# Storing one tile's blocks earlier and turning q in two halves, in a linear attention and expert kernel

## The chip, the cores and the metric

The kernel runs on one core of a Trainium2 chip. The metric is the device time of one execution in microseconds (us). Five engines work side by side and meet at semaphores: TensorE (PE) multiplies, VectorE (DVE), ScalarE (ACT) and GpSimd (POOL) compute elementwise, and SyncE (SP) issues most of the transfers (DMAs). Each engine takes its instructions strictly in the order in which the program lists them.

## The reference

Eight batches of linear attention, whose output is the input of four experts that every row goes through:

```python
# q, k, v: (8, 8 heads, 576, 64)
phi = lambda x: np.where(x > 0, x, np.exp(x) - 1.0) + 1.0
q_p, k_p = phi(q), phi(k)
kv  = einsum('bhsd,bhse->bhde', k_p, v);  z = sum(k_p, axis=2)
num = einsum('bhsd,bhde->bhse', q_p, kv)
den = einsum('bhsd,bhd->bhs', q_p, z)[..., None] + 1e-06
x = (num / den) as rows of 8 * 64            # 4608 x 512
# domain_probs: (4608, 4), w1: (4, 512, 1024), w2: (4, 1024, 512)
p = domain_probs / (domain_probs.sum(-1, keepdims=True) + 1e-09)
out = sum over e of p[:, e:e+1] * (maximum(x @ w1[e], 0.0) @ w2[e])
```

## The kernel before

**Tiles.** A tile is 512 rows of `x`: 512 of the 576 rows of one batch; the 64 left over of each of the eight batches make a ninth tile (`xT_left`). Tiles run in the order 0 to 6, the ninth, 7. While the experts of one tile run on PE, the attention of the next batch runs on the other engines and in gaps that are made for it in PE's order, so that its `x` is ready, transposed, when the next tile begins.

**The experts of a tile.** For each of the four experts, layer 1 (`Block`, lines 875 to 949) and layer 2 (`layer2_product`, line 807; for tile 0 `layer2_part`, line 732) run as blocks of four or eight matmuls. Both layers after tile 0 use a scheme with seven products in place of eight, for which POOL makes sums (`hidden_sum`, `token_sum`). A result of layer 2 is added into `acc`, a block of 128 rows by 512: the first time by ACT (line 726), after that by DVE (line 728). A tile has four such blocks. `acc` has five buffers (`NACC`), and one of them serves a piece of q early in the program. When the last expert's part is added, the block is stored by a DMA that SP issues (`store`, line 709); the buffer is free for another block when that store has landed.

**The attention of a batch.** q, k and v come as four pieces each (two heads, 256 KB) into a ring of six buffers (`raw`, lines 324 to 342), and the 64 rows left over in separate small loads ("rests", `load_left`, line 310, two DMAs each for k, v and q). ACT and DVE compute phi in two steps: `phi_act` (lines 364 and 367) writes x + 1 into `kp` or `qp` and exp(x) into PSUM, `phi_dve` (line 372) combines them. `kv` multiplies. q has to be turned (transposed) to be a weight of PE: for batches 2 to 7 one DMA transposes all of `qp` into `qT` (`dma_qT`, line 410); for batch 1 PE does it (`pe_qT`, line 445). `nd` (line 487) multiplies `qT` by `kvz` in six groups of three, each followed by a division on DVE into `x_sb`; `dma_xT` turns each finished pair of heads into the next tile's `xT`.

**The order.** Every step is a named generator, put at a position counted in slots (56 slots a tile, from `CFG["ATTN"]` for the attention), and the steps are sorted by position: that is the order of instructions on each engine. For the first two tiles, up to a part of batch 3's steps, the order is written out by hand, `CFG["EARLY"]`: each appearance of a name advances its generator to the next `yield`. So `y3.23`, layer 2 of tile 0 for expert 3, block 2, part 3, appears three times: matmuls, the addition on DVE, the store. Names that matter here: `y3.03`, `y3.13`, `y3.23`, `y3.33` (blocks 0 to 3 of tile 0); `m10.21` and the like (tile 1, expert 0, product 2, half 1); `b2.q1` and `b2.qm1` (batch 2, `phi_act` and `phi_dve` of q's piece 1); `b2.load3` (a load into the ring); `b1.next` (the rests of batch 2); `b2.qT` (turning); `b2.nd0` (first group of numerators).

Of the kernel before, what the change touches and what calls it, by code (L numbers as in the profile page):

```python
# [12 lines left out]
FP16 = mybir.dt.float16  # L13
# [17 lines left out]
            v=(18.1, 19.16, 22.55, 30.55),  # L31
            k=(-5.5, 26.3, 27.5, 28.5),
# [5 lines left out]
            q=(36.4, 36.95, 40.2, 43.4),  # L38
            qd=(37.75, 39.0, 40.55, 44.7),
            lq=54.05,  # L40
            lqd=54.5,
# [9 lines left out]
            v=(4.4, 8.7, 12.1, 14.8),  # L51
            k=(0.3, 2.9, 6.7, 11.25),
# [5 lines left out]
            q=(20.1, 22.1, 27.0, 30.0),  # L58
            qd=(21.75, 27.2, 30.2, 32.3),
            lq=33.9,  # L60
            lqd=38.3,
            qT=35.9,
            nd=(39.3, 40.4, 42.0, 43.5, 45.3, 46.1),
            nl=52.1,
        ),
# [1 line left out]
            v=(4.4, 8.7, 12.1, 14.8),  # L67
            k=(0.3, 2.9, 6.7, 11.25),
# [5 lines left out]
            q=(20.1, 22.1, 27.0, 30.0),  # L74
            qd=(21.75, 27.2, 30.2, 32.3),
            lq=23.3,
            lqd=24.4,
            qT=35.9,
            nd=(39.3, 40.4, 42.0, 43.5, 45.3, 46.1),
            nl=37.2,  # L80
        ),
# [53 lines left out]
    ),  # L135
}

# [2 lines left out]
def kernel(  # L140
# [10 lines left out]
    nc = tc.nc  # L151
    ATTN, HSUM, L2ORD, L2AT = (CFG[x] for x in ("ATTN", "HSUM", "L2ORD", "L2AT"))

    B, H, S, D = q.shape
# [72 lines left out]
    def aps(shape, dtype, name, more=""):  # L227
        return ppm.tile(shape, dtype, tag=CFG["BANK"].get(now[0] + more, "s"), bufs=2, name=name)
# [67 lines left out]
    class Batch:  # L296
# [59 lines left out]
        def phi_act(self, name, i):  # L356

            if name == "k" and self.kp is None:
                self.kp = pa.tile([P, CM, H, D], FP16, tag="kp", bufs=1, name="kp")
            if name == "q" and self.qp is None:  # L360
                self.qp = pa.tile([P, CM, H, D], FP16, tag="kp", bufs=1, name="qp")
            src = self.raw[name, i]
            dst = (self.qp if name == "q" else self.kp)[:, :, i * HQ : (i + 1) * HQ, :]
            nc.scalar.activation(dst.rearrange("p c h d -> p h c d"), src, AF.Identity, bias=1.0)
            ee = aps([P, HQ * CM * D], FP32, "psum_ee")
            ee = ee.rearrange("p (c h d) -> p c h d", c=CM, h=HQ)
            nc.scalar.activation(ee.rearrange("p c h d -> p h c d"), src, AF.Exp)
            self.ph[name, i] = dst, ee
# [38 lines left out]
                    out=dst, in0=dst, scalar=1.0, in1=el[us], op0=AO.max, op1=AO.min  # L407
                )

        def dma_qT(self):  # L410
            if self.qT is None:
                self.qT = pa.tile([P, CM, NPAIR, P], FP16, tag="qT", bufs=1, name="qT")
            nc.sync.dma_start_transpose(
                out=self.qT.rearrange("p c a i -> p (c a) i"),
                in_=self.qp.rearrange("p c h d -> p (c h d)"),
            )

        def dma_qTl(self):
# [25 lines left out]

        def pe_qT(self, pair, eng=nc.vector):
            ps = aps([P, CM, P], FP16, "psum_qT")
            for c in range(CM):
                nc.tensor.transpose(
                    out=ps[:, c], in_=self.qp[:, c, 2 * pair : 2 * pair + 2], identity=identh
                )  # L450
            yield
            if self.qT is None:
                self.qT = pa.tile([P, CM, NPAIR, P], FP16, tag="qT", bufs=1, name="qT")
            (eng.copy if eng is nc.scalar else eng.tensor_copy)(out=self.qT[:, :, pair], in_=ps)

        def kv(self):
            ps = aps([P, NPAIR, DE], FP32, "psum_kv")
# [29 lines left out]
        def nd(self, i0, n):  # L487

            ps = aps([P, 3, 2, DE], FP32, "psum_nd")
            for i in range(n):  # L490
                pair, c = divmod(i0 + i, CM)
                nc.tensor.matmul(  # L492
                    out=ps[:, i],
                    lhsT=self.qT[:, c, pair],
                    rhs=self.kvz[:, pair],
                    start=True,
                    stop=True,
                )
            yield
            if self.x is None:  # L500
                x = pa.tile([P, CM, H, DE], FP16, tag="vp", bufs=1, name="x_sb")
                x = x.rearrange("p c h d -> p (c h d)")[:, 0 : NPAIR * CM * P]
                self.x = x.rearrange("p (a c i) -> p a c i", c=CM, i=P)
            self.norm(self.x.rearrange("p a c i -> p (a c) i")[:, i0 : i0 + n], ps, n)
# [450 lines left out]
    def batch_steps(bt, nxt, put, at, at_next):  # L955
# [6 lines left out]
            if m < len(later):  # L962
                (bt if m < len(mine) else nxt).load(*later[m])

        def load_left():
            if nxt is not None:
                nxt.alloc_left()
                nxt.load_left("k", "v", "q")

        b = bt.b  # L970

# [19 lines left out]
            put(at["l" + n], f"b{b}.l{n}", bt.left_act, n)  # L991
            put(at["l" + n + "d"], f"b{b}.l{n}m", bt.left_dve, n)
        put(at["kv"], f"b{b}.kv", bt.kv)
        put(at["lqd"] + 1, f"b{b}.next", load_left)
        if not first:
            put(at["lqd"] + 2, f"b{b}.qTl", bt.dma_qTl)
        if first:
            put(at["qtl"], f"b{b}.qTl", bt.pe_qTl)
            for i in range(NPAIR):
                put(at["qt"][i], f"b{b}.qT{i}", bt.pe_qT, i, nc.scalar)  # L1000
                for hf in range(2):
                    put(at["nd"][i], f"b{b}.nd{i}{hf}", bt.nd, i * CM + 2 * hf, 2)
                put(at["xt"][i], f"b{b}.xT{i}", bt.pe_xT if i == 2 else bt.dma_xT, i)
            for i in range(NRAW):
                put(at["next"][i], f"b{b}.load{i}", load, len(mine) + i)
        else:
            put(at["qT"], f"b{b}.qT", bt.dma_qT)
            for i in range(6):
                put(at["nd"][i], f"b{b}.nd{i}", numerators, 3 * i, min(3, NPAIR * CM - 3 * i))
        if nxt is None or b in (1, 4):  # L1010
# [17 lines left out]
    with tc.manual_schedule(  # L1028
# [76 lines left out]
        for j in range(0, NTILES - 1):  # L1105
            at = base + 2 * NSLOT * E * (j - 1) if j else 0.0

            def put(pos, *g, at=at):
                put_at(at + pos, *g)
# [65 lines left out]
```

## Time and profile before

| | |
|---|---|
| median of three runs | 486.1 us |
| the three runs | 484.93, 486.1, 487.2 us |
| the profiled execution | 484.29 us |
| its span, first to last instruction | 482.5 us |
| granted clock of PE | 0.999 |

Lines of a profile read so: the start in us from the span's start and the duration, the engine (SPq is SP's queue of issues, PEld the loading of weights into PE), the line of the kernel, the operation, what it writes and what it reads, the shapes, the number of instructions merged, and in brackets how long the engine stood idle before and what ended that by the profile's inference. Lines on DMAs give the number of issues, the size of one and the median time from issue to landing. A table by stretches gives the window, its length, then the busy time (and the number of instructions) of PE, PEld, DVE, ACT and POOL, PE's granted clock, the busy share of the DMA engines and their GB/s.

### The profile page before, as it was taken

Reading aid. Unit: us, or ns where it says so; the run is one execution under the profiler, and the core shown is the slowest. Engines: PE = TensorE matmul, PEld = TensorE weight load, DVE = VectorE, ACT = ScalarE, POOL = GpSimd, SP = SyncE. Lnnn points to the kernel's source line nnn. Section 1 sums busy time; section 2 is a strip of 40 time slices with the busy share of each in tenths; the row PEclk is TensorE's granted clock in tenths of the full one; section 3 lists DMA queues with packets and bytes.
Section 4 is the critical chain, followed back from the end, with each engine's and each line's share of the span. In section 5 each row is a group of like instructions: output and inputs, shape, how many; then the busy total and the mean of one; then the engine's idle time right before and its main releaser. Section 6 shows DMA issues by size and latency. Waiting matters only on the chain.

```text
span 482.5 us, 12014 instructions
## 1 busy us (share of the span) xinstructions
PE 475.3 (98%) x4565; PEld 407.1 (84%) x4565; DVE 379.1 (79%) x794; ACT 329.8 (68%) x659; POOL 358.8 (74%) x343
## 2 busy tenths in 40 slices
PE   8999999999999999999999999999999999999997
PEld 3776757898889888998889888988898888888886
DVE  5868998897968796888678885988787756775677
ACT  5688969956795599649874888478954465446540
POOL 5566144788966986789777976697769877987775
PEclk9999999999999999999999999999999999999999
DMA  8999997533445155524552346423230020003002
GB/s 293 218 218 259 234 200 234 154 84 88 132 145 108 43 157 160 122 59 117 178 135 57 109 131 161 83 67 113 67 70 13 1 88 1 1 2 88 2 1 87
DMA packets 80297, 54.06 MB, mean 112 GB/s; under 512 B 45344, under 2 KB 72992, under 8 KB 80240
## 3 DMA queue, kind: packets, MB, share of 16 engines
q1 hardware_dynamic: 70096, 40.89, 31.3%
q0 software_dynamic: 8896, 11.34, 12.1%
q10 hardware_dynamic: 1248, 1.08, 0.7%
q8 instruction: 35, 0.57, 0.5%
q14 instruction: 22, 0.18, 0.1%
HBM read 45.16 MB, written 9.44 MB: 113 GB/s over the span
## 4 chain that ended last, share of the span: by engine, by line
PE 94%; DMA 2%; DVE 2%; ACT 1%; issue 0%; SPq 0%; ACTq 0%
PE py L832 38%; PE pb L889 25%; PE pe L889 19%; PE py L737 6%; PE ph L677 1%; PE psum_nd L492 1%; DMA rawq<-in_q_dram 1%; PE psum_kv L464 1%; DMA out_dram<-acc 1%; PE pb L832 1%; PE pe L832 1%; PE psum_nl L511 0%; DVE acc L728 0%; DVE kpos L588 0%; ACT ee L603 0%; ACT acc L726 0%
## 5 line engine op out<-in xcount | busy, mean ns | idle before, releaser
L728 DVE SCALAR_TENSOR_TENSOR acc<-py,p_sb,acc 128x256 f32<-128x256 f32 (+1 forms) x382 | 182.1, 488 | 43.9 <-PE py L832 39.4
L873 DVE CUSTOM_DVE_ANT_0 h<-pe,u 128x512 f16<-128x512 f32 x140 | 96.0, 688 | 43.3 <-PE pe L889 22.5
L889 PEld LDWEIGHTS <-w 128*128 128x128 f16 x1120 | 109.0, 98 | 16.1
L799 POOL TENSOR_TENSOR hs<-h 128x512 f16<-128x512 f16 x64 | 73.8, 1154 | 56.0 <-DVE h L873 44.3
L832 PEld LDWEIGHTS <-h 128*128 128x128 f16 x1024 | 99.9, 98 | 12.3 <-issue 0.9
L832 PE MATMUL py<-w,h 128*128 128x256 f16 x744 | 106.5, 273 | 0.6 <-ACT acc L726 0.6
L900 ACT COPY u<-pb 128x512 f32<-128x512 f32 x140 | 82.7, 592 | 30.9 <-PE pb L889 28.6
L801 POOL TENSOR_TENSOR hs<-hs,h 128x512 f16<-128x512 f16 x64 | 74.3, 1160 | 24.9 <-PE py L832 22.3
L889 PEld LDWEIGHTS <-s 128*128 128x128 f16 x840 | 81.4, 98 | 11.6
L889 PE MATMUL pb<-tt,w 128*128 128x256 f16 x560 | 83.9, 273 | 0.0
L832 PEld LDWEIGHTS <-hs 128*128 128x128 f16 x768 | 74.3, 98 | 8.9 <-issue 0.2
L805 POOL TENSOR_TENSOR hs<-h,hs 128x512 f16<-128x512 f16 x64 | 74.7, 1167 | 1.2 <-POOL h L803 0.7
L803 POOL TENSOR_TENSOR h<-h 128x512 f16<-128x512 f16 x64 | 74.3, 1161 | 0.1
L832 PE MATMUL py<-t,hs 128*128 128x256 f16 x496 | 74.1, 273 | 0.0
L922 ACT ACTIVATE h<-pe 128x512 f16<-128x512 f32 x70 | 42.1, 601 | 41.8 <-PE pe L889 41.3
L915 ACT COPY pe<-pb 128x512 f32<-128x512 f32 x70 | 40.0, 573 | 39.8 <-PE pb L889 14.5
L943 ACT ACTIVATE h<-pb 128x512 f16<-128x512 f32 x70 | 41.9, 600 | 5.4 <-PE pb L889 5.4
L889 PE MATMUL pb<-tt,s 128*128 128x256 f16 x280 | 41.8, 273 | 0.0
L889 PE MATMUL pe<-tt,s 128*128 128x256 f16 x280 | 41.8, 273 | 0.0
L889 PE MATMUL pe<-xT,s 128*128 128x256 f16 x248 | 37.1, 273 | 0.0
L889 PE MATMUL pe<-xT,w 128*128 128x256 f16 x248 | 37.1, 273 | 0.0
L889 PE MATMUL pb<-xT,w 128*128 128x256 f16 x248 | 36.9, 273 | 0.0
(134 smaller groups left out, 594.8 us busy)
## 6 DMA issues: line engine op xcount, KB each, us to landing
w<-in_moe_w_dram POOLq DMA_DIRECT2D x14, 512.0 KB, 10.4
out_dram<-acc SPq DMA_DIRECT2D x28, 256.0 KB, 2.5
rawb<-in_k_dram SPq DMA_DIRECT2D x24, 256.0 KB, 3.1
rawb<-in_q_dram SPq DMA_DIRECT2D x24, 256.0 KB, 2.6
rawb<-in_v_dram SPq DMA_DIRECT2D x24, 256.0 KB, 2.7
out_dram<-acc SPq DMA_DIRECT2D x12, 128.0 KB, 2.3
w<-in_moe_w_dram POOLq DMA_DIRECT2D x4, 256.0 KB, 5.4
rawb<-in_k_dram POOLq DMA_DIRECT2D x4, 256.0 KB, 10.5
```

The costliest lines, as they stand in the source:

```text
L728: nc.vector.scalar_tensor_tensor(out=acc, in0=ps, scalar=pscal, in1=acc, op0=AO.mult, op1=AO.add)
L799: nc.gpsimd.tensor_tensor(out=hs[0], in0=a21, in1=a22, op=AO.add)
L801: nc.gpsimd.tensor_tensor(out=hs[1], in0=hs[0], in1=a11, op=AO.subtract)
L803: nc.gpsimd.tensor_tensor(out=a21, in0=a11, in1=a21, op=AO.subtract)
L805: nc.gpsimd.tensor_tensor(out=hs[3], in0=a12, in1=hs[1], op=AO.subtract)
L832: nc.tensor.matmul(out=ps, lhsT=lhsT(k), rhs=rhs[:, k], start=first and k == 0, stop=k == FH - 1, skip_group_check=True,)
L873: nc.vector._custom_dve(TENSOR_ADD_SAT, out=out, in0=ps, in1=u, s0=BIG, s1=0.0)
L889: nc.tensor.matmul(out=ps[:, kk], lhsT=lk(kc), rhs=rhs[:, kc], start=first and kk == 0 and kc == 0, stop=kc == 1, skip_group_check=True,)
L900: nc.scalar.copy(u, self.b)
L915: nc.scalar.copy(self.e5, self.b)
L922: nc.scalar.activation(self.h[:, :, 0, 0:NH], self.e5, AF.Relu)
L943: nc.scalar.activation(self.h[:, :, 1, 0:NH], self.b, AF.Relu)
```

## The change

Three edits. (1) In the hand-written order the stores of tile 0's blocks 2 and 3, which stood behind the addition to block 0 and behind the store of block 1, follow the addition to their own block at once. (2) For batches 2 to 7, `qp` and `qT` are laid out as two halves of four heads, and each half is turned by a DMA of its own; from batch 3 on the first stands right behind q's second piece (27.25, its `phi_dve` is at 27.2), the second right behind q's fourth piece (32.35 against 32.3), where one DMA stood at 35.9. In batch 2 both stand where the one stood. Batch 1's `pe_qT` and the numerators use the new layout. (3) The rests of q are a step of their own, `nextq`; for batch 2 it stands behind six loads of that batch's pieces, for later batches right behind the rests of k and v.

```diff
-            qT=35.9,
+            qT=(27.25, 32.35),
...
     "EARLY"  (only what differs)
- b1.load4 b1.load3 b1.load2 ... b1.load5 b2.load0
+ b1.load4 b1.load3 b1.load2 ... b1.load5 b1.nextq b2.load0
- y2.13 b2.km0 t2.0 t2.1 y3.23 b2.load3 b2.lkm
+ y2.13 b2.km0 t2.0 t2.1 y3.23 y3.23 b2.load3 b2.lkm
- b2.load10 y3.33 b2.km2 pr1
+ b2.load10 y3.33 y3.33 b2.km2 pr1
- hs10.13 y3.03 y3.23 b2.load7
+ hs10.13 y3.03 b2.load7
- b2.lqm y3.33 b2.qT b2.nd0
+ b2.lqm b2.qT0 b2.qT1 b2.nd0
- m11.10 m11.10 b2.next m11.61
+ m11.10 m11.10 b2.next b2.nextq m11.61
...
-                self.qp = pa.tile([P, CM, H, D], FP16, tag="kp", bufs=1, name="qp")
+                self.qp = pa.tile([P, 2, CM, HG, D], FP16, tag="kp", bufs=1, name="qp")
             src = self.raw[name, i]
-            dst = (self.qp if name == "q" else self.kp)[:, :, i * HQ : (i + 1) * HQ, :]
+            if name == "q":
+                dst = self.qp[:, i // 2, :, i % 2 * HQ : (i % 2 + 1) * HQ]
+            else:
+                dst = self.kp[:, :, i * HQ : (i + 1) * HQ]
...
-        def dma_qT(self):
+        def new_qT(self):
+            self.qT = pa.tile([P, 2, CM, 2, P], FP16, tag="qT", bufs=1, name="qT")
+
+        def dma_qT(self, g):
             if self.qT is None:
-                self.qT = pa.tile([P, CM, NPAIR, P], FP16, tag="qT", bufs=1, name="qT")
+                self.new_qT()
             nc.sync.dma_start_transpose(
-                out=self.qT.rearrange("p c a i -> p (c a) i"),
-                in_=self.qp.rearrange("p c h d -> p (c h d)"),
+                out=self.qT[:, g].rearrange("p c a i -> p (c a) i"),
+                in_=self.qp[:, g].rearrange("p c h d -> p (c h d)"),
             )
...
-                    lhsT=self.qT[:, c, pair],
+                    lhsT=self.qT[:, pair // 2, c, pair % 2],
...
-        def load_left():
+        def load_left(*names):
             if nxt is not None:
-                nxt.alloc_left()
-                nxt.load_left("k", "v", "q")
+                nxt.load_left(*names)
...
-        put(at["lqd"] + 1, f"b{b}.next", load_left)
+        put(at["lqd"] + 1, f"b{b}.next", load_left, "k", "v")
+        put(at["lqd"] + 1.001, f"b{b}.nextq", load_left, "q")
...
-            put(at["qT"], f"b{b}.qT", bt.dma_qT)
+            for g in range(2):
+                put(at["qT"][g], f"b{b}.qT{g}", bt.dma_qT, g)
```

More of the change, by code (lines that the diff above doesn't have):

```diff
@@ L77 @@
             lqd=24.4,
-            qT=35.9,
+            qT=(27.25, 32.35),
             nd=(39.3, 40.4, 42.0, 43.5, 45.3, 46.1),
@@ L446, in pe_qT @@
             ps = aps([P, CM, P], FP16, "psum_qT")
+            g, a = divmod(pair, 2)
             for c in range(CM):
                 nc.tensor.transpose(
-                    out=ps[:, c], in_=self.qp[:, c, 2 * pair : 2 * pair + 2], identity=identh
+                    out=ps[:, c], in_=self.qp[:, g, c, 2 * a : 2 * a + 2], identity=identh
                 )
@@ L452, in pe_qT @@
             if self.qT is None:
-                self.qT = pa.tile([P, CM, NPAIR, P], FP16, tag="qT", bufs=1, name="qT")
-            (eng.copy if eng is nc.scalar else eng.tensor_copy)(out=self.qT[:, :, pair], in_=ps)
+                self.new_qT()
+            (eng.copy if eng is nc.scalar else eng.tensor_copy)(out=self.qT[:, g, :, a], in_=ps)
         def kv(self):
```

35 rows, old and new, of the table nl are left out of this document.

## The prediction

> **What bounds the kernel now.** I read the page first, then the busy time by stretches, cut where TensorE (PE) is not full, then each engine in order of time around the two cuts, and last the margins of the transfers that the change moves. The page:
>
> ```profile
> span 482.5 us, 12014 instructions
> PE 475.3 (98%) x4565; PEld 407.1 (84%) x4565; DVE 379.1 (79%) x794; ACT 329.8 (68%) x659; POOL 358.8 (74%) x343
> ```
>
> The busy time of each engine by stretches (PE first):
>
> ```profile
> 24.00:84.00 60.00, 60.00 (x509) 41.28 (x507) 52.41 (x99) 52.45 (x107) 26.77 (x33) 1.00 1.06 228
> 84.00:96.00 12.00, 11.77 (x110) 10.38 (x109) 10.58 (x19) 10.94 (x26) 8.87 (x8) 1.00 0.63 168
> 96.00:288.00 192.00, 192.00 (x1935) 171.93 (x1933) 157.33 (x345) 142.37 (x287) 157.09 (x144) 1.00 0.42 114
> 288.00:300.00 12.00, 11.66 (x108) 10.31 (x107) 7.78 (x15) 10.57 (x24) 8.39 (x8) 1.00 0.55 154
> 300.00:468.00 168.00, 168.00 (x1594) 150.63 (x1592) 123.25 (x258) 98.58 (x189) 135.00 (x122) 1.00 0.17 45
> ```
>
> PE is busy in every microsecond from 24 to 468 but for two places, and its clock is granted in full (1.00). The change adds and removes no instruction of PE. So in this execution it can only win back those two places, or open new ones. In the last row 1594 matmuls fill 168.00 us, 0.105 us each, so a group of four fills 0.42 us. PE in order of time at the two places:
>
> ```profile
> 89.70 0.60 PE L889 MATMUL pe<-xT,s 128*128 128x256 f16 x4
> 90.53 0.60 PE L832 MATMUL py<-w,h 128*128 128x256 f16 x4 [0.23 <-ACT acc L726]
> ...
> 292.17 0.60 PE L889 MATMUL pb<-xT,w 128*128 128x256 f16 x4
> 293.11 0.60 PE L832 MATMUL py<-w,h 128*128 128x256 f16 x4 [0.34 <-ACT acc L726]
> ```
>
> From start to start the first pair takes 0.83 us, 0.41 more than its four matmuls need; the second takes 0.94 us, 0.52 more. Both wait for ScalarE (ACT) writing `acc`. Together 0.93 us, 0.2% of the time. ACT at the same places:
>
> ```profile
> 87.20 0.64 ACT L900 COPY u<-pb 128x512 f32<-128x512 f32 x1
> 88.61 0.48 ACT L726 ACTIVATE acc<-py,p_sb 128x256 f32<-128x256 f32 x1 [0.76 <-PE pe L889]
> 90.02 0.46 ACT L726 ACTIVATE acc<-py,p_sb 128x256 f32<-128x256 f32 x1
> ...
> 292.58 0.47 ACT L726 ACTIVATE acc<-py,p_sb 128x256 f32<-128x256 f32 x1 [0.90 <-DMA out_dram<-acc]
> ```
>
> ACT stood 0.76 us before the step at 88.61. The view blames a PE product, but that step reads `py`, not `pe`: an `acc` buffer is the thing it can have lacked. At 292.58 the view names the store outright.
>
> **Edit 1, tile 0's stores.** `acc` has five buffers, tile 0 fills four, one more was used for a piece of q. Tile 1's fourth block (the step at 88.61, after those of `m10.21`, `m10.51` and `m10.20`) needs a fourth free buffer, so a third of tile 0's stores must have landed. VectorE's (DVE) last additions to blocks 2, 3 and 1 of tile 0, in that order, then SyncE's queue (SP), then the landings of the stores issued at 81.20 and at 84.60:
>
> ```profile
> 71.68 0.74 DVE L728 SCALAR_TENSOR_TENSOR acc<-py,p_sb,acc 128x512 f32<-128x512 f32 x1
> 75.27 0.74 DVE L728 SCALAR_TENSOR_TENSOR acc<-py,p_sb,acc 128x512 f32<-128x512 f32 x1
> 83.79 0.75 DVE L728 SCALAR_TENSOR_TENSOR acc<-py,p_sb,acc 128x512 f32<-128x512 f32 x1 [0.24 <-PE py L737]
> ```
>
> ```profile
> 79.31 0.37 SPq L339 DMA_DIRECT2D rawb<-in_v_dram  x1
> 81.20 0.84 SPq L709 DMA_DIRECT2D out_dram<-acc  x2
> ...
> 84.60 0.89 SPq L709 DMA_DIRECT2D out_dram<-acc  x2
> ```
>
> ```profile
> out_dram<-acc SPq DMA_DIRECT2D x1, 256.0 KB, 2.1
> out_dram<-acc SPq DMA_DIRECT2D x1, 256.0 KB, 3.9
> ```
>
> Block 2 is complete at 72.42 and block 3 at 76.01, yet their stores leave second of the pairs at 81.20 and 84.60. The earliest store of the second pair lands at 84.60 + 3.9 = 88.5; ACT starts at 88.61. That is the wait. After the change the store of block 2 stands ahead of the load of q's piece 1, and that of block 3 right behind the load issued at 79.31: it leaves at 79.7, since its addition is long done, and lands at 81.8 to 83.6 (2.1 to 3.9 us). Three stores have then landed before 85, so the step at 88.61 can start when ACT is free, at 87.20 + 0.64 = 87.84. The next `acc` step moves from 90.02 towards 89.25, 0.76 us, more than the 0.41 that PE loses: that gap goes. PE is full right behind it, so all 0.41 us reaches the end, until another wait takes it.
>
> The two stores wait for nothing on SP when their turn comes, so what queues behind them (loads of q's pieces 1 and 3 and of batch 3) leaves at most one issue time later, some 0.4 us a store (0.84 for two). Cost taken: 0. The nearest consumer is ACT's step on q's piece 3 (SP, ACT, and the page's row of q's loads):
>
> ```profile
> 75.44 3.72 SPq L339 DMA_DIRECT2D rawb<-in_q_dram  x3
> ...
> 82.98 0.63 ACT L364 ACTIVATE qp<-rawb 128x512 f16<-128x512 f32 x1
> ...
> rawb<-in_q_dram SPq DMA_DIRECT2D x24, 256.0 KB, 2.6
> ```
>
> The last of these three issues ends at 79.16; with the median 2.6 us to landing, piece 3 is there at 81.4 to 81.8 for a use at 82.98. If the cover of 1.2 us were gone, the cost would be the excess over it, times the share of an ACT wait that PE feels (0.41 of 0.76).
>
> The Trainium skill (DMA: Bandwidth & Descriptors, Latency and other measured facts) says that most of a DMA's fixed cost is the memory's receipt, 0.2 us on average and 2 us under high load. That speaks against putting a store among loads: by it, an estimate of 1.8 us more would bring piece 3 up to 0.6 us late, and the sum would lose 0.3 us of the 0.41. The landings above (2.1 against 3.9 us with other transfers close by) agree in kind; how much a load suffers no run here shows.
>
> **Edit 2, q turned in halves.** For batch 5, as for the others from 3 on:
>
> ```profile
> 292.94 0.67 DVE L372 SCALAR_TENSOR_TENSOR qp<-qp,psum_ee 128x512 f16<-128x512 f16 x1
> ```
>
> ```profile
> 297.23 2.72 SPq L413 DMA_TRANSPOSE qT<-qp  x1
> ```
>
> ```profile
> qT<-qp SPq DMA_TRANSPOSE x6, 4.6
> xT<-x_sb SPq DMA_TRANSPOSE x27, 2.4
> ```
>
> ```profile
> 302.61 0.26 PEld L492 LDWEIGHTS <-qT 128*128 128x128 f16 x3
> ```
>
> The whole q (16 blocks of 128x128) lands at 297.23 + 4.6 = 301.8, 0.8 us ahead of its first use at 302.61. Half 0 can leave at 292.94 + 0.67 = 293.6. Nothing shows a transpose of 8 blocks; it lies between the 4 blocks of `xT` (2.4 us to landing) and the 16 (4.6). I take 3.1, in proportion to blocks. Half 0 then lands at 296.7, 5.9 us ahead of use; half 1, still issued near 297.2, at 300.3, and its first use is the third group of numerators, later than 302.61. On SP each half holds the queue for 1.2 us (`xT`, shown below) to 2.7, so 1.7 in proportion; the load of the next batch that stands behind half 0 is a tile from its use. Six transposes more, no PE work, no new wait before a full engine: 0 in this execution. Without the 0.8 us of margin the gain would be what PE had waited.
>
> Batch 2's steps are in the hand-written order, and both halves stand behind all of its q:
>
> ```profile
> 90.87 1.84 SPq L413 DMA_TRANSPOSE qT<-qp  x1
> ...
> 96.06 0.33 PE L492 MATMUL psum_nd<-kvz,qT 128*128 128x130 f16 x3
> ```
>
> Half 0 lands near 94.0 against 96.06 needed; half 1 leaves near 92.6 and lands at 95.0 to 97.2, for use from the third group on. Cost 0.
>
> The new places of `qp` and `qT` leave 128 contiguous elements in every row that an engine writes or reads; only strides change. Cost 0.
>
> **Edit 3, q's rests.** From batch 3 on only one name moves by 0.001 slots, with no SP step between. For batch 2 two issues move behind six loads:
>
> ```profile
> 66.49 1.28 SPq L317 DMA_DIRECT2D rl<-in_q_dram  x2
> ...
> 69.53 0.42 SPq L339 DMA_DIRECT2D rawb<-in_k_dram  x1
> ```
>
> ```profile
> rawb<-in_k_dram SPq DMA_DIRECT2D x1, 256.0 KB, 4.7
> ```
>
> ```profile
> 74.30 0.63 ACT L364 ACTIVATE kp<-rawb 128x512 f16<-128x512 f32 x1
> ```
>
> The k piece issued at 69.53 lands at 74.2, used at 74.30: 0.1 us of margin. It now leaves up to 1.28 us earlier. No wait is seen on it, so 0 here. The rests themselves are used over 20 us later.
>
> **The sum.** The profiled execution took 484.29 us, its span of 482.5 and 1.79 around it. Less 0.41 it is 483.9. The median of the three runs is 486.1, 1.81 above the profiled one. What fills that is not shown. It can be stalls at just the margins of 0.1 and 0.8 us that edits 2 and 3 widen, or something untouched: the edits' share lies between 0 and 1.81. I take half, 0.9, since the margins are thinner than the difference between two landings of one kind (2.1 and 3.9), while the trace shows no PE wait there. 486.1 - 0.41 - 0.9 = 484.8 us.
>
> **Rivals.** First, all hidden stalls go: the median comes down to the profiled execution, and the wait at 292.58 goes too, 484.29 - 0.93 = 483.4, 0.6% faster. For it: two margins near zero, and each edit lies at one. Against: the store behind 292.58 is tile 3's, which the change does not move.
>
> Second, it does not do what it says: block 1's store, issued at 84.60 and not moved, is what ACT waited for, or something new takes the 0.41: 486.1. Its landing fits as well as a fourth buffer does, but a third store landed early makes it unneeded.
>
> Third, slower: `qp` is one tile. If its accesses were ordered by the tile and not by the half, ACT's writing of q's piece 3 would wait for half 0's transpose to land.
>
> ```profile
> 295.31 0.65 ACT L364 ACTIVATE qp<-rawb 128x512 f16<-128x512 f32 x1
> ```
>
> That would be 296.7 - 295.3 = 1.4 us of ACT. ACT waits of 0.76 and 0.90 us cost PE 0.41 and 0.52, about 0.55 of the wait, so 0.8 us a tile, in batches 3 to 7: 4.0 us, 486.1 - 0.4 + 4.0 = 489.7. It decides once the wait is over some 0.35 us, what ACT's 0.76 left unfelt. Against it stands `x_sb`, also one tile: DVE writes it at 307.98, half a microsecond after a transpose of another part was issued, long before the 2.4 us to landing, and does not wait:
>
> ```profile
> 307.47 1.21 SPq L546 DMA_TRANSPOSE xT<-x_sb  x1
> ```
>
> ```profile
> 307.98 0.56 DVE L480 TENSOR_TENSOR x_sb<-psum_nd,recip 128x384 f16<-128x384 f32 x1
> ```
>
> **How the numbers follow.** 0.5%, 2.4 us, is about what a measurement of this kernel can tell from no change. The forecast at 484.8 has 0.45, the first rival 0.25, the second 0.20, the third 0.10. Forecast and second rival are within 0.5%: 0.65. Faster is the first, 0.25; slower the third, 0.10. The range takes in all but the third. Its ends allow for the runs: the first rival's 483.4 less 0.3, half of the 0.64 between the two fastest readings (484.29 and 484.93), gives 483.1; the second's end is the slowest run of before, 487.2.
>
> **What would show it.** Right: no idle time of ACT before the fourth `acc` step of tile 1, four stores of tile 0 leaving at about 76, 80, 81 and 85, PE full from 84 to 96, `qT` halves landing over 4 us ahead of their first use. Wrong: ACT steps L364 or DVE steps L372 on `qp` waiting for a DMA; ACT waiting for `rawb` between 75 and 90; a span that differs by more than 1 us while PE shows no new or lost gap.

## The result and the profile after

The changed kernel takes 484.23 us (median of 13 runs, 483.22 to 484.51), the kernel before 485.68 us (13 runs, 484.17 to 487.2). The ratio is 0.9968, with a 95% interval of 0.9956 to 0.9979: 0.3% faster, 1.45 us. The spread shrank too, from 3.0 us to 1.3. The profiled execution of the changed kernel took 483.89 us; its span:

```profile
span 482.1 us, 12029 instructions
```

Against the profiled execution of before (484.29 us) that is only 0.4 us less. That this equals the 0.41 us of the first edit is chance: by the table of losses below, the changed execution loses 0.45 us less ahead of the numerators of batch 2 and 0.50 us less near the end, but 0.23 us more in between and some 0.3 us more elsewhere. The rest of the 1.45 us must lie in what other executions of before lose and its profiled one did not. A second profile of the unchanged kernel, below, shows such losses.

Busy time by stretches of the changed kernel (window, length, then PE, PEld, DVE, ACT, POOL):

```profile
84.00:96.00 12.00, 12.00 (x116) 10.78 (x114) 10.87 (x19) 11.44 (x26) 9.33 (x8) 1.00 0.61 152
288.00:300.00 12.00, 12.00 (x113) 10.73 (x111) 7.54 (x15) 11.07 (x25) 8.81 (x9) 1.00 0.72 180
```

PE is full in both stretches in which it was not: 12.00 against 11.77 and 11.66. The same two pairs of PE instructions, in order of time:

```profile
89.87 0.60 PE L897 MATMUL pe<-xT,s 128*128 128x256 f16 x4
90.30 0.60 PE L840 MATMUL py<-w,h 128*128 128x256 f16 x4
...
292.11 0.60 PE L897 MATMUL pb<-xT,w 128*128 128x256 f16 x4
292.54 0.60 PE L840 MATMUL py<-w,h 128*128 128x256 f16 x4
```

From start to start they now take 0.43 us each, where they took 0.83 and 0.94. The first is the edit's doing. The second is not: in a second profile of the unchanged kernel it is gone too (the column "to the end" of the table below, 0.50 and 0). ACT and SP around the first place (L734 is the step on `acc`, L717 the store, L340 the loads of pieces, L318 the rests; in the changed kernel lines stand 1 to 8 further down):

```profile
87.38 0.64 ACT L908 COPY u<-pb 128x512 f32<-128x512 f32 x1
87.89 0.50 ACT L734 ACTIVATE acc<-py,p_sb 128x256 f32<-128x256 f32 x1
```

```profile
68.38 0.42 SPq L340 DMA_DIRECT2D rawb<-in_k_dram  x1
...
69.87 0.61 SPq L318 DMA_DIRECT2D rl<-in_q_dram  x1
...
75.95 0.42 SPq L717 DMA_DIRECT2D out_dram<-acc  x1
...
79.81 1.92 SPq L717 DMA_DIRECT2D out_dram<-acc  x2
...
84.76 0.42 SPq L717 DMA_DIRECT2D out_dram<-acc  x1
```

The step on `acc` starts as soon as ACT is free, at 87.89, where ACT had stood idle 0.76 us. The stores leave at 76, 80 to 81 and 85. The load of k that ACT needs next leaves at 68.38 in place of 69.53.

### The profile page after: what moved, and what is told of

It reads as the page before. It is cut to its first block, busy times and chain, and to the rows that moved or that the text cites. A ratio compares the mean times of both kernels' runs of the same rounds, so it can differ in the third digit from the quotient of the medians.

```text
span 482.1 us, 12029 instructions
## 1 busy us (share of the span) xinstructions
PE 476.2 (99%) x4565; PEld 406.7 (84%) x4565; DVE 379.1 (79%) x794; ACT 329.9 (68%) x659; POOL 358.8 (74%) x343
## 3 DMA queue, kind: packets, MB, share of 16 engines
q10 hardware_dynamic: 1248, 1.08, 0.7%
## 4 chain that ended last, share of the span: by engine, by line
PE 93%; DMA 2%; POOL 2%; DVE 1%; ACT 1%; issue 1%; SPq 0%; POOLq 0%
PE py L840 38%; PE pb L897 25%; PE pe L897 19%; PE py L745 6%; PE ph L685 1%; PE psum_nd L500 1%; DMA rawq<-in_q_dram 1%; DMA xT<-x_sb 1%; PE psum_kv L472 1%; PE pb L840 1%; POOL tt L878 1%; PE pe L840 1%; POOL hs L813 0%; POOL hs L807 0%; PE psum_nl L519 0%
```

## The experiments

The theory going in was the prediction's: ACT waits for a buffer of `acc`, which edit 1 frees; what else is gained are waits that most executions have and the first profile missed, at margins that edits 2 and 3 widen. Rivals: only the stores matter; only the halves of q; or it is not the buffer but the traffic of the stores. Twelve kernels were run (two of them the kernel before and the changed one once more), in three groups, each group on one chip beside the kernel before (484.4 to 485.4 us there). A ratio is to the kernel before of the same group.

The profiles of all of them are read in one table first. PE's starts mark three intervals that hold the same work in every kernel: from the last `psum_xT` transpose of batch 1 to the first numerators (`psum_nd`) of batch 2, from there to the first numerators of batch 3, and from there to the last matmul. The shortest seen are 29.54, 53.53 and 328.63 us; what a kernel has beyond them is PE's loss. The two columns of ACT are its idle time ahead of the step on batch 2's third piece of k (near 75 us) and ahead of the step on `acc` near 88 us, from ACT in order of time. All in us:

| kernel | profiled | ACT waits for k | ACT waits for `acc` | PE loss to numerators of batch 2 | to those of batch 3 | to the end |
|---|---|---|---|---|---|---|
| before | 484.29 | 0 | 0.76 | 0.46 | 0.01 | 0.50 |
| before, again | 484.89 | 0.89 | 1.08 | 1.60 | 0.27 | 0 |
| edit 1 alone | 485.27 | 1.22 | 0 | 1.48 | 0.33 | 0.38 |
| edit 2 alone | 485.40 | 1.09 | 0.49 | 1.33 | 0.11 | 0.83 |
| edit 2 alone, again | 484.92 | 1.12 | 0.90 | 1.66 | 0 | 0 |
| edit 3 alone | 485.33 | 0 | 1.33 | 1.02 | 0.13 | 0.67 |
| without edit 1 | 484.47 | 1.08 | 0.58 | 1.33 | 0 | 0.07 |
| without edit 3 | 484.19 | 0.45 | 0 | 0.71 | 0 | 0.41 |
| without edit 2 | 484.65 | 0 | 0 | 0.01 | 0.32 | 1.00 |
| changed | 483.89 | 0 | 0 | 0.01 | 0.24 | 0 |
| changed, again | 483.59 | 0 | 0 | 0.01 | 0.02 | 0 |
| edit 3 and block 3's store | 483.81 | 0 | 0 | 0.18 | 0.19 | 0.82 |
| edit 3 and block 2's store | 483.73 | 0 | 0.57 | 0.27 | 0 | 0.36 |
| edit 1 and q's piece 0 behind | 483.73 | 0 | 0 | 0 | 0 | 0 |

The profiled times differ by 1.8 us; less the three losses they differ by 1.1 (482.6 to 483.7), so the losses are a part of the differences, not all of them. In three rows ACT also waits 0.4 to 0.9 us for batch 2's second piece of k, near 67 us (edit 1 alone, edit 3 with block 3's store, q's piece 0 behind); two of these rows lose only 0.18 us and nothing up to the numerators. One profile a kernel cannot carry a verdict; the ratios do that, and the table says where to look.

### The kernel before, again

No edit.

> The kernel before, unchanged, as a second sample of its own profile. All theories: ratio 1.000 within 0.15%. Theory S (the stores): a wait of ACT before the fourth acc step of tile 1 near 88.6 us, with 0.3 to 0.6 us lost by PE behind it, as in the first profile. Theory M (margins: what the median has above the profiled execution are PE waits for qT or ACT waits for rawb): if this execution is one of the longer ones (over 485 us), a wait of PE before the first numerators of some tile, or of ACT for rawb between 72 and 79 us, of 0.3 us or more in sum.

Measured 485.62 us, ratio 1.0002 (0.9988 to 1.0015). Its profiled execution took 484.89. Stretches, then ACT in order of time, then the load it names (the DMAs issued near 69.3):

```profile
72.00:84.00 12.00, 11.56 (x119) 8.17 (x117) 10.61 (x20) 10.99 (x24) 4.78 (x4) 1.00 0.71 223
84.00:96.00 12.00, 11.70 (x106) 10.00 (x105) 11.12 (x18) 10.86 (x25) 8.48 (x7) 1.00 0.61 158
```

```profile
74.86 0.63 ACT L364 ACTIVATE kp<-rawb 128x512 f16<-128x512 f32 x1 [0.89 <-DMA rawb<-in_k_dram]
...
89.46 0.47 ACT L726 ACTIVATE acc<-py,p_sb 128x256 f32<-128x256 f32 x1 [1.08 <-DMA out_dram<-acc]
```

```profile
69.31 0.42 SPq L339 DMA_DIRECT2D rawb<-in_k_dram  x1
```

```profile
rawb<-in_k_dram SPq DMA_DIRECT2D x1, 256.0 KB, 5.5
```

There are two waits, one after the other on ACT. The piece of k, issued at 69.31 as before, took 5.5 us to land in place of 4.7: the margin of 0.1 us has become a wait of 0.89 us. The wait for `acc` follows, and this time the view names the store outright. PE is short of both stretches, by 0.44 and 0.30 us, and loses 1.60 us by its starts (the two differ because the ends of matmuls are modelled and cover part of a gap). A part of what the first profile of before hid is found.

### Each edit alone

Edit 1 alone:

```diff
- t2.1 y3.23 b2.load3 ... b2.load10 y3.33 b2.km2 ... y3.03 y3.23 b2.load7 ... b2.lqm y3.33 b2.qT
+ t2.1 y3.23 y3.23 b2.load3 ... b2.load10 y3.33 y3.33 b2.km2 ... y3.03 b2.load7 ... b2.lqm b2.qT
```

> Edit 1 alone (the stores of tile 0's blocks 2 and 3 behind their own additions). Theory S: takes 0.4 us in every execution, ratio 0.999, and if the wait at 88.6 us is larger in most executions than in the profiled one, up to the whole 1.45 us (0.997). Theory M: 0.4 us and no more, since qT and the k pieces keep their margins; the spread of the runs stays at some 2 us. Profile: ACT's step at 88 starts without a wait, PE full from 84 to 96.

Measured 484.87 us, ratio 0.9988 (0.9974 to 1.0002). Stretches and ACT:

```profile
72.00:84.00 12.00, 11.23 (x118) 8.04 (x116) 10.16 (x20) 10.66 (x24) 5.05 (x5) 1.00 0.71 213
84.00:96.00 12.00, 12.00 (x109) 10.26 (x107) 11.59 (x18) 11.41 (x26) 8.88 (x7) 1.00 0.63 169
```

```profile
75.28 0.63 ACT L365 ACTIVATE kp<-rawb 128x512 f16<-128x512 f32 x1 [1.22 <-DMA rawb<-in_k_dram]
```

The wait for `acc` is gone, PE is full from 84 on. The wait for k is whole.

Edit 2 alone, run twice (the second time in the third group):

```diff
- qT=35.9,
+ qT=(27.25, 32.35),
- b2.lqm y3.33 b2.qT b2.nd0
+ b2.lqm y3.33 b2.qT0 b2.qT1 b2.nd0
  (and the layout of qp and qT in two halves)
```

> Edit 2 alone (q turned in two halves, earlier). Theory S: no change, ratio 1.000, the wait near 88.6 us stays. Theory M by qT: 0.5 to 1 us faster, ratio 0.998 to 0.999, and a narrower spread. Profile: qT's first half lands over 5 us ahead of its first use in batches 3 to 7, PE still loses about 0.4 us near 90.

> Edit 2 alone once more, beside the three above. Theory that edit 2 brings nothing (edits 1 and 3 alone were as fast as the changed kernel): 1.000 of before within 0.12%, with the losses near 76 and 90 in its profile. Rival (the 0.998 of its first run is real): 0.998 again.

Measured 484.89 us, ratio 0.9981 (0.9966 to 0.9996), and then 485.25 us, ratio 1.0003 (0.9991 to 1.0015). The first interval lies wholly below 1, the second does not repeat it. Both profiles have both waits; ACT in the second:

```profile
75.17 0.63 ACT L368 ACTIVATE kp<-rawb 128x512 f16<-128x512 f32 x1 [1.12 <-DMA rawb<-in_k_dram]
```

Nothing in this profile is better than in before, again, and the first run's gain is not counted as one.

Edit 3 alone:

```diff
- b1.load4 b1.load3 b1.load2 ... b1.load5 b2.load0
+ b1.load4 b1.load3 b1.load2 ... b1.load5 b1.nextq b2.load0
- nxt.load_left("k", "v", "q")
+ nxt.load_left(*names)      # "k", "v" in next, "q" in nextq
```

> Edit 3 alone (the rests of q of batch 2 behind six loads). Theory S: no change, 1.000. Theory M by the k pieces of batch 2: 0.5 to 1 us faster, 0.998 to 0.999. Profile: the k piece used at 74.3 us lands 1 us or more ahead of its use instead of 0.1.

Measured 484.55 us, ratio 0.9985 (0.9973 to 0.9997). Stretches, ACT, SP, and the DMA issued at 84.78:

```profile
72.00:84.00 12.00, 12.00 (x126) 8.72 (x125) 10.85 (x22) 11.67 (x25) 4.62 (x4) 1.00 0.68 202
84.00:96.00 12.00, 11.37 (x105) 9.88 (x103) 10.06 (x17) 10.51 (x24) 8.33 (x7) 1.00 0.63 161
```

```profile
89.35 0.47 ACT L727 ACTIVATE acc<-py,p_sb 128x256 f32<-128x256 f32 x1 [1.33 <-DMA out_dram<-acc]
```

```profile
84.78 0.89 SPq L710 DMA_DIRECT2D out_dram<-acc  x2
```

```profile
out_dram<-acc SPq DMA_DIRECT2D x1, 256.0 KB, 4.5
```

Now PE is full up to 84, and the second wait is 1.33 us, the longest of all. The landing of block 1's store (84.78 + 4.5 = 89.3) ends it at 89.35. In before, again it ended at 89.46, nearly the same, but by another way. There the wait for k had delayed DVE's last addition to block 1, and with it the store. DVE and SP in before, again, the landing of the store issued at 85.57, then DVE in edit 3 alone:

```profile
84.80 0.74 DVE L728 SCALAR_TENSOR_TENSOR acc<-py,p_sb,acc 128x512 f32<-128x512 f32 x1
```

```profile
85.57 1.96 SPq L709 DMA_DIRECT2D out_dram<-acc  x2
```

```profile
out_dram<-acc SPq DMA_DIRECT2D x1, 256.0 KB, 3.8
```

```profile
83.97 0.75 DVE L729 SCALAR_TENSOR_TENSOR acc<-py,p_sb,acc 128x512 f32<-128x512 f32 x1 [0.23 <-PE py L738]
```

Without the wait for k the store leaves 0.8 us earlier, and this one then took 4.5 us to land in place of 3.8. The delay is in all profiles: that addition ends 18.5 to 18.7 us after the last `psum_xT` of batch 1 in the eight without the wait for k, and 19.3 to 20.1 us in the six with it. So the first wait moves the end of the second, and how long a store takes to land (3.2 to 4.5 us in the profiles where ACT waits for one) sets the rest. Up to the numerators of batch 2 PE loses 1.02 us here and 1.60 in before, again, so these two profiles differ by 0.58 us.

### One edit left out

The changed kernel with one of the three edits undone, as the diffs above backwards, and the changed kernel once more as the yardstick of this group.

> Edits 2 and 3 without edit 1 (the stores as before). Theory of three waits (the k pieces near 75 us cost PE up to 1.3 us, the stores near 90 us cost 0.4 to 1.0 us, qT costs nothing): PE loses 0.4 to 1.0 us near 90 and nothing near 76; 0.4 to 0.9 us slower than the changed kernel, about 0.998 of before. Rival (edit 2 brings as much as the others, since it shortens SP's queue or frees transfers for the later stores near 292 and 344 us): the same loss near 90, but no loss near 292 and 344.

> Edits 1 and 3 without edit 2 (q turned whole). Theory of three waits: the same as the changed kernel within 0.1%, 0.997 of before, PE full from 72 to 96, and qT lands 0.6 to 0.9 us ahead of its use without any PE wait. Rival (edit 2 counts): 0.5 to 1 us slower than the changed kernel, with PE losses of 0.3 us or more at 292 or 344 us or before the first numerators of a tile.

> Edits 1 and 2 without edit 3 (the rests of q ahead of batch 2's pieces). Theory of three waits: ACT waits for a k piece near 75 us, PE loses 0.8 to 1.3 us between 72 and 84 in a typical execution, nothing near 90; 0.5 to 1 us slower than the changed kernel. Rival: within 0.1% of the changed kernel.

> The changed kernel once more, beside the three above on one chip. All theories: 0.997 of before within 0.15%. Theory of three waits: PE full from 72 to 96; what is left over are losses of 0.2 to 0.5 us near 124, 292 or 344 us, which come and go between executions. Rival: no loss at 292 and 344 either.

| kernel | median us | ratio to before | 95% interval |
|---|---|---|---|
| changed, again | 483.34 | 0.9972 | 0.9961 to 0.9983 |
| without edit 1 | 484.51 | 0.9998 | 0.9986 to 1.0010 |
| without edit 2 | 483.32 | 0.9975 | 0.9963 to 0.9987 |
| without edit 3 | 484.70 | 1.0003 | 0.9991 to 1.0015 |

Edits 1 and 3 together are the whole gain, and without either of them nothing of it can be measured. Edit 2 adds nothing. Stretches of the kernel without edit 2, then of the one without edit 3:

```profile
84.00:96.00 12.00, 12.00 (x115) 10.81 (x114) 10.71 (x20) 11.42 (x27) 9.33 (x8) 1.00 0.59 148
```

```profile
72.00:84.00 12.00, 11.78 (x122) 8.55 (x121) 10.87 (x20) 11.43 (x25) 5.19 (x5) 1.00 0.77 238
```

The profile of the kernel without edit 2 is of its slowest execution (484.65 us against a median of 483.32) and loses 1.00 us to the end, which is what the rival of edit 2 expected there. The time speaks against that rival, and the column does not bear it out either: 0 to 1.00 us in the eight profiles with q turned whole, 0 to 0.83 in the six with halves.

The kernel without edit 1 holds a surprise: it has edit 3, and ACT waits for k all the same. SP, the load issued there, and ACT:

```profile
67.81 0.42 SPq L340 DMA_DIRECT2D rawb<-in_k_dram  x1
```

```profile
rawb<-in_k_dram SPq DMA_DIRECT2D x1, 256.0 KB, 7.1
```

```profile
74.94 0.63 ACT L368 ACTIVATE kp<-rawb 128x512 f16<-128x512 f32 x1 [1.08 <-DMA rawb<-in_k_dram]
```

The load left at 67.81, 1.7 us earlier than in before, and took 7.1 us in place of 4.7. The wait stands in five of the six profiles that have neither edit 3 nor the moved load of q, and in one of the seven with edit 3: the edit makes it rarer, it doesn't end it.

What one edit brings by itself is not settled. By the first group it is 0.12% and 0.15% for edits 1 and 3, with 1 just inside and just outside the interval; in time that is 0.50 and 0.82 us, which add up to about what the pair brings (1.08 to 1.45 us). By the second group it is nothing, since with only one of the two done (and edit 2) the ratio is 0.9998 or 1.0003. The intervals are 1.2 to 1.4 us wide, so it cannot be said whether the two prices add.

### The buffer or the traffic

Edit 3 with the store of only one block moved. By the buffer theory the fourth `acc` step of tile 1 needs any third store landed; if it is traffic, what matters is how many bytes are in flight around 85.

```diff
  edit 3, and block 3 alone:
- b2.load10 y3.33 b2.km2 ... b2.lqm y3.33 b2.qT
+ b2.load10 y3.33 y3.33 b2.km2 ... b2.lqm b2.qT
  edit 3, and block 2 alone:
- y3.23 b2.load3 ... y3.03 y3.23 b2.load7
+ y3.23 y3.23 b2.load3 ... y3.03 b2.load7
```

> Edit 3 and, of edit 1, the store of block 3 alone (block 2's stays second of its pair at 81.6). Buffer theory (tile 1's fourth acc block lacks a buffer until a third store of tile 0 has landed): block 3's store lands near 82 to 84.5, three have landed before 85, so ACT does not wait near 88 and PE loses nothing there: the same as edits 1 and 3 together, 0.9975 of before. Rival (it is the transfers around 82 to 86 that delay block 1's store): half of edit 1's gain, since one of two stores is out of the way: a wait of ACT of 0.5 us or so stays.

> Edit 3 and, of edit 1, the store of block 2 alone (block 3's stays behind that of block 1, at 85). Buffer theory: only two stores have landed before 88, as before the change, so ACT's wait near 88.6 and 0.4 to 1 us of PE stay: the same as edit 3 alone. Rival (transfers around 82 to 86): half of edit 1's gain, the wait shorter by a half.

Measured 483.76 us, ratio 0.9970 (0.9957 to 0.9983) with block 3's store; 484.05 us, ratio 0.9977 (0.9967 to 0.9987) with block 2's. SP and ACT of the first:

```profile
79.05 2.46 SPq L710 DMA_DIRECT2D out_dram<-acc  x3
```

```profile
87.16 0.49 ACT L727 ACTIVATE acc<-py,p_sb 128x256 f32<-128x256 f32 x1
```

With three stores issued by 81.5 ACT does not wait. SP, the DMA issued at 84.38, and ACT of the second:

```profile
75.57 0.42 SPq L710 DMA_DIRECT2D out_dram<-acc  x1
...
84.38 1.90 SPq L710 DMA_DIRECT2D out_dram<-acc  x2
```

```profile
out_dram<-acc SPq DMA_DIRECT2D x1, 256.0 KB, 3.7
```

```profile
88.20 0.48 ACT L727 ACTIVATE acc<-py,p_sb 128x256 f32<-128x256 f32 x1 [0.57 <-DMA out_dram<-acc]
```

Here only two stores were issued before 84.38, and ACT waits until 88.20 for the first of the pair (84.38 + 3.7 = 88.1). The same holds in all seven profiles in which ACT waits for `acc`: its step starts 0.1 us after the third store of tile 0 has landed. In the seven others three stores have landed before ACT comes. So the buffer decides whether there is a wait. The length of the wait goes by the store's landing, 3.7 us here and 4.5 with edit 3 alone; whether less traffic made it shorter is not shown. The times do not tell the two kernels apart (their intervals overlap), and the second did better than the buffer theory expected: 0.9977, where edit 3 alone had 0.9985, with a wait shorter by more than a half, as the rival had it. A sixth buffer, which would have asked the question without moving a store, was not run.

### The rests, or what stands ahead of k

Edit 1, with the rests left where they were and the load of q's piece 0 (256 KB) moved behind instead:

```diff
- b1.next b2.load2 b2.load1 b1.load4 ... b1.load5 b2.load0
+ b1.next b2.load1 b1.load4 ... b1.load5 b2.load2 b2.load0
```

> Edit 1, the rests of q as before, but the load of q's piece 0 of batch 2 (256 KB, first used at 81 us) moved from ahead of five loads to behind them, another transfer out of the way of the same k pieces. Theory of the k pieces (they land late because of what is queued ahead of them on SP and on the DMA engines): the k piece that is used at 74.3 lands near 73, PE is full from 72 to 96, and the time is that of edits 1 and 3, 0.9975 of before. Rival (the rests themselves matter, by their 256-byte rows or by holding the buffer of the rests): the loss of 0.9 to 1.3 us near 76 stays, 1.000 to 0.999.

Measured 483.95 us, ratio 0.9975 (0.9961 to 0.9989). ACT:

```profile
74.57 0.63 ACT L365 ACTIVATE kp<-rawb 128x512 f16<-128x512 f32 x1
```

No wait ahead of it. The load of that piece and its landing:

```profile
69.34 0.42 SPq L340 DMA_DIRECT2D rawb<-in_k_dram  x1
```

```profile
rawb<-in_k_dram SPq DMA_DIRECT2D x1, 256.0 KB, 3.6
```

It left no earlier than in before, again (69.31), but landed after 3.6 us in place of 5.5: here the landing itself was shorter, with q's piece out of the way. The kernel does as much as the changed one did in its own groups (0.9968, 0.9972), so the rests are nothing special: another transfer taken from ahead of k does as well. No kernel of the twelve beat the changed one beyond the intervals.

## Why the prediction was right, step by step

**The time.** 484.8 was predicted and 484.23 measured, from a level of before that was 485.68 rather than the 486.1 of the three runs shown. The fall was 1.45 us against 1.3. The sign and the size held. The split of the sum did not, and that the size came out is in part luck: the 0.9 was half of a 1.81 whose cause was not known. By the thirteen runs the median of before lies 485.68 - 484.29 = 1.39 us above the profiled execution, and of the two margins that were to fill it only one did.

**Edit 1, 0.41 us.** The steps are as predicted: stores at 76, 80, 81 and 85, no idle time before the fourth `acc` step, PE full from 84 to 96. The landings were sized too short: block 3's store, taken at 2.1 to 3.9 us, took 4.7, and the third store landed at 84.8, still 3 us ahead of ACT. The second rival, that block 1's store was what ACT waited for, fell. It is issued at 84.76 in the changed kernel; the DMA issued there:

```profile
out_dram<-acc SPq DMA_DIRECT2D x1, 256.0 KB, 3.9
```

It lands at 88.7, after ACT has begun at 87.89. In before it was indeed block 1's store that ACT waited for, but as the third to leave; in the changed kernel it is the fourth, and not needed. The size, though, was that of one execution. In the others with the stores of both blocks unmoved the wait is 0.49 to 1.33 us of ACT. PE's loss can be read by itself only where there is no wait for k: 0.46 us in before, 1.02 in edit 3 alone.

**Edit 2, 0 and a share of the hidden 0.9.** The 0 was right; the share was wrong. None of the kernels that turn q whole shows PE waiting for `qT`. SP's transposes and PE's first use in the kernel without edit 2 (SP, DMA, PEld):

```profile
296.89 2.15 SPq L414 DMA_TRANSPOSE qT<-qp  x1
```

```profile
qT<-qp SPq DMA_TRANSPOSE x1, 4.5
```

```profile
302.27 0.26 PEld L493 LDWEIGHTS <-qT 128*128 128x128 f16 x3
```

It lands at 301.4, 0.9 us ahead of use. The margin was 0.6 to 1.5 us in the eight profiles of the kernels that turn q whole, never less. The prediction took the two margins of 0.1 and 0.8 us as alike because landings of one kind differed by 1.8; the first was overrun in five of six profiles, the second in none. The halves in the changed kernel (all issues of the line, with the row of their landings):

```profile
L420 SPq DMA_TRANSPOSE qT<-qp x12: 1231/1232/1327, 90.2 to 347.3; - x12
...
DMA to landing us min/median/max: 3.0/3.2/4.3
```

1.23 us on SP (1.7 estimated) and 3.2 us to landing (3.1 estimated). In batches 3 to 7 each half lands 4.3 to 5.8 us ahead of its own first use, as foretold; in batch 2, where both stand where the one stood, it is 2.2 and 4.0 us.

**Edit 3, 0 in that execution.** Right for it, and the margin of 0.1 us was the hidden wait: 0.89 to 1.22 us of ACT in before again, in edit 1 alone and in both runs of edit 2, 0.45 in the kernel without edit 3. What failed is the way in which the 0.9 was shared out: it was given to the margins of `qT` and of k alike, and edit 1 was held at the 0.41 of one execution. The runs give `qT` nothing, show the margin of k as a wait of most executions, and give edit 1 more than 0.41 in some. How the 1.45 us divide between edits 1 and 3 stays open. The two waits are not independent, since the wait for k also delays the store that ends the other, but whether their prices add no run here decides: the edits alone gave 0.50 and 0.82 us in one group, and each edit left out cost the whole gain in another.

**Loads among stores.** The piece 3 of q, the nearest consumer behind the moved stores (SP, the DMA, ACT):

```profile
78.83 0.37 SPq L340 DMA_DIRECT2D rawb<-in_q_dram  x1
```

```profile
rawb<-in_q_dram SPq DMA_DIRECT2D x1, 256.0 KB, 4.0
```

```profile
83.15 0.63 ACT L368 ACTIVATE qp<-rawb 128x512 f16<-128x512 f32 x1
```

It took 4.0 us against the median of 2.6, and was there at 82.8 for a use at 83.15. The Trainium skill (DMA: Bandwidth & Descriptors, Latency and other measured facts) puts most of a transfer's fixed cost into the memory's receipt, longer under load, from which the prediction had estimated 1.8 us more. The 1.4 us seen agree in kind with that, and 0.3 us of the cover of 1.2 were left: the cost of 0 held, narrowly. It was no accident of one profile. The same load took 3.8 to 4.2 us in all six profiles with both stores moved and 2.6 to 3.2 in the six with neither; in edit 1 alone it landed in the very moment of its use, 83.96 for 83.98.

**The rivals.** The first (483.4, every hidden wait goes and the one at 292 too) overshot: the edits don't move the store that ACT waits for at 292, and the column "to the end" shows losses of up to 1.0 us, there and near 344, in kernels with and without each edit. The third (slower, if accesses to `qp` were ordered by the whole tile) fell. SP, then ACT and DVE in the changed kernel:

```profile
293.61 1.23 SPq L420 DMA_TRANSPOSE qT<-qp  x1
```

```profile
294.52 0.63 ACT L368 ACTIVATE qp<-rawb 128x512 f16<-128x512 f32 x1
```

```profile
295.23 1.28 DVE L376 SCALAR_TENSOR_TENSOR qp<-qp,psum_ee 128x512 f16<-128x512 f16 x2
```

Half 0's transpose leaves at 293.61 and needs 3 us to land; ACT and DVE write the other half meanwhile, without waiting.

## What to carry to other kernels

A margin of 0.1 us in one profiled execution was a wait in five of six profiles of kernels that left it as it was. So profile the unchanged kernel a second time before putting a price on an edit, and compare a margin with how far that same landing moves, not with landings in general. When an engine meets two waits one after the other, look at what each does to the end of the other: here the first also delayed the store that ended the second. Don't take it as given that their prices add, or that they don't. Leave each edit out of the whole change as well as trying it alone, and keep to what both agree on: here that edits 1 and 3 together are the gain and that edit 2 adds nothing.

## What the runs showed of the hardware

The same load of 256 KB (batch 2's third piece of k) took 3.6 to 7.1 us to land in the fourteen profiles: 4.7 and 5.5 in the two of the kernel before, 4.2 in the changed kernel. The longest was the one issued earliest (67.81, without edit 1), the shortest the one with q's piece 0 out of its way. Within the time around it (70.9 to 72.5 us) the DMA engines of before, again also carried one packet of 16 KB of another queue, which the profile names "instruction". Such a packet is seen near there in the other profiles too, some 1 to 2 us later in those with edit 3. That it delays the load is not shown: nothing was run that moves it alone.
